# Two attention layers and two gated MLPs on one core: the kernel rebuilt around chunks of 512 tokens

## The chip, the cores and the metric

The kernel runs on one core of one Trainium2 chip. The core has a matrix engine (TensorE, PE in the profile; its weight loads are shown apart as PEld), a vector engine (VectorE, DVE), an engine for functions of one variable (ScalarE, ACT), a general engine (GpSimd, POOL) and an engine that mostly issues transfers (SyncE, SP). Matrix products land in PSUM, a small memory of eight banks per partition, a bank holding 512 fp32 numbers; everything else lives in SBUF, and the inputs lie in HBM. The metric is the device time of one execution in microseconds (us).

## The reference, cut to what matters

The input x has 2048 tokens of 1024 features in bf16. A linear attention layer (A) and a gated MLP (B) are applied in turn, twice, with the same weights, each on the layernorm of x and added to it.

```python
def _A_ref(x, wqkv, wo):                      # H = 32 heads of 32 features
    q, k, v = split(x @ wqkv)                 # 1024 -> 3 x 1024
    phi = lambda t: jnp.where(t > 0, t + 1, jnp.exp(t)) + 1e-6
    pq, pk = phi(q), phi(k)
    kv = jnp.einsum("bhsd,bhse->bhde", pk, v) # 32x32 per head, over all tokens
    z = jnp.einsum("bhsd->bhd", pk)
    num = jnp.einsum("bhqd,bhde->bhqe", pq, kv)
    den = jnp.einsum("bhqd,bhd->bhq", pq, z)[..., None] + 1e-6
    return (num / den) @ wo

def _B_ref(x, W_gate, W_up, W_down):          # F = 3584
    gate, up = x @ W_gate, x @ W_up
    gate = gate * (gate > 0)
    return (gate * up) @ W_down

x = x + _A_ref(_layernorm(x), A_wqkv, A_wo)
x = x + _B_ref(_layernorm(x), B_W_gate, B_W_up, B_W_down)
x = x + _A_ref(_layernorm(x), A_wqkv, A_wo)
x = x + _B_ref(_layernorm(x), B_W_gate, B_W_up, B_W_down)
```

## The kernel before

The tokens are cut into 16 tiles of 128. The residual x is held in SBUF in fp32 for the whole run (`x_sb`); it is read in bf16 and cast at the start, and cast back and written at the end.

`_layernorm_T` (lines 17 to 44) normalizes one tile: statistics on DVE (L25, L27), variance plus epsilon on DVE (L29), a square root on ACT (L30), a reciprocal on DVE (L31), the normalized tile in bf16 on DVE (L33), eight 128x128 transposes on PE (L39), and two copies out of PSUM, one on ACT (L42) and one on DVE (L44).

`_phi` (lines 47 to 53) makes max(t, 0) + exp(min(t, 0)) + 1e-6 out of a PSUM tile in four instructions, DVE, ACT, DVE, ACT.

`_layer_A` has two stages. In the first, for each tile, k and v are made from the transposed tile and a weight slab of 4 MB (L112, 32 matmuls of 128x512 per tile), k goes through `_phi`, and v is copied out with a column of ones behind each group of 128 features (L120). `kv_step` then makes, for eight groups of 128 features, pk times v together with pk's sums (L92), and adds them to an fp32 sum in SBUF on DVE (L97). At the stage's end the sum is masked to the 32x32 blocks of the heads (L128), and a matrix `zrep` is built that holds the sums in the same block form (L131). In the second stage, for each chunk of 512 tokens and each group of 128 features, q is made (L165), goes through `_phi`, and `nd_step` makes numerator and denominator by one matmul each per 256 tokens (L150, L152); ACT adds epsilon to the denominator (L155), DVE takes its reciprocal (L157) and multiplies (L158). Eight groups make a chunk, and the chunk is multiplied by wo and added to x (L179, L183). The weights of the second stage lie in another pool, which is loaded when the first stage's is given up.

`_layer_B` takes the tokens in two halves of 1024. For each half, gate and up are made for 28 blocks of 128 features (L227), the gate goes through a Relu on ACT (L231), and DVE multiplies (L232). Then W_down is applied in seven groups of four feature blocks; after each group the partial sums are added to x on DVE (L243, L247). Weights stream through pools with two buffers; the loads are issued on SP's queue and on ACT's. The first half's eight tiles are normalized before its matmuls, the second half's within the first half's down stage.

The order of the instructions on each engine is the scheduler's of the tile framework: the order of the program is a priority, and an instruction that is ready may be taken ahead of one that isn't. Buffers of a pool are given again when their last reader is done; a load or a write into one waits for that.

## Time and profile before

| | |
|---|---|
| time, median of 3 runs | 1966.81 us (1965.41 to 1966.97) |
| profiled execution, span from the first to the last instruction | 1957.3 us |
| what lies around the span (median less span) | 9.5 us |
| mean granted TensorE clock | 0.960 of full speed |
| PE, DVE, ACT busy | 1747.4, 1133.1, 502.6 us |
| HBM read, written | 109.05 MB, 4.19 MB |

The profile is one execution, with a record for each instruction; the page has no time of its own for that execution other than its span, so the time of the runs is set beside it. A row of a group gives line, engine, operation, output and inputs with their shapes, count, then busy us, mean ns of one, then the idle time of the engine just before and what ended it. A row of a window gives start and end, length, busy us and count for PE, PEld, DVE, ACT and POOL, the granted clock, the share of time that the 16 DMA engines were busy, and GB/s. Matmuls overlap in a pipeline, so the mean of one (379 ns for 128x512) is longer than their pace.

### The profile page before, as it was taken

Reading aid. Unit: us, or ns where it says so; the run is one execution under the profiler, and the core shown is the slowest. Engines: PE = TensorE matmul, PEld = TensorE weight load, DVE = VectorE, ACT = ScalarE, POOL = GpSimd, SP = SyncE. Lnnn points to the kernel's source line nnn. Section 1 sums busy time; section 2 is a strip of 40 time slices with the busy share of each in tenths; the row PEclk is TensorE's granted clock in tenths of the full one; section 3 lists DMA queues with packets and bytes.
Section 4 is the critical chain, followed back from the end, with each engine's and each line's share of the span. In section 5 each row is a group of like instructions: output and inputs, shape, how many; then the busy total and the mean of one; then the engine's idle time right before and its main releaser. Section 6 shows DMA issues by size and latency. Waiting matters only on the chain.

```text
span 1957.3 us, 21219 instructions
## 1 busy us (share of the span) xinstructions
PE 1747.4 (89%) x8282; PEld 809.6 (41%) x8448; DVE 1133.1 (58%) x1863; ACT 502.6 (26%) x853; POOL 21.2 (1%) x54
## 2 busy tenths in 40 slices
PE   6995777699999999999979957666999999999998
PEld 3452333244444444444434423333444444444443
DVE  7856999841117822117786679998322288212277
ACT  5852433321110011110067524333111100111100
POOL 1000000000000000000000000000000000000000
PEclk9998888899999999999999978998999999999999
DMA  4002000042222222211120020002332313232112
GB/s 172 1 1 86 0 1 1 2 135 80 76 75 67 84 71 80 76 54 52 57 86 2 1 86 1 1 1 62 90 86 66 87 65 114 81 85 66 44 65 87
DMA packets 142886, 114.64 MB, mean 59 GB/s; under 512 B 3520, under 2 KB 118208, under 8 KB 142784
## 3 DMA queue, kind: packets, MB, share of 16 engines
q1 hardware_dynamic: 72448, 58.73, 9.6%
q10 hardware_dynamic: 70336, 54.53, 9.1%
q8 instruction: 66, 1.08, 0.2%
q14 instruction: 36, 0.29, 0.0%
HBM read 109.05 MB, written 4.19 MB: 58 GB/s over the span
## 4 chain that ended last, share of the span: by engine, by line
PE 72%; DVE 16%; ACT 4%; issue 4%; DMA 3%; POOL 0%; SPq 0%; POOLq 0%; ACTq 0%; DVEq 0%
PE pu L227 19%; PE pg L227 19%; PE ps L243 19%; DVE rd L157 8%; PE ps L112 7%; PE ps L179 4%; DVE oT L158 2%; DVE m L51 1%; DVE m L49 1%; DMA xin<-in_A_x_dram 1%; DMA wq<-in_A_wqkv_dram 1%; PE ps L165 1%; ACT L50 1%; DVE xn L33 1%; DVE stats L25 1%
## 5 line engine op out<-in xcount | busy, mean ns | idle before, releaser
L232 DVE TENSOR_TENSOR hT<-pu,rg 128x512 bf16<-128x512 f32 x224 | 154.8, 691 | 598.4 <-PE pu L227 581.7
L227 PE MATMUL pg<-xnT_h,wg 128*128 128x512 bf16 x1758 | 421.5, 379 | 3.6 <-DVE xnT_h L44 1.9
L227 PE MATMUL pu<-xnT_h,wu 128*128 128x512 bf16 x1752 | 421.2, 379 | 2.2
L243 PE MATMUL ps<-wd,hT 128*128 128x512 bf16 x1754 | 387.4, 379 | 2.0
L247 DVE TENSOR_TENSOR x_sb<-x_sb,ps 128x512 f32<-128x512 f32 x448 | 305.8, 687 | 68.6 <-PE ps L243 66.7
L231 ACT ACTIVATE rg<-pg 128x512 f32<-128x512 f32 x224 | 133.7, 597 | 623.9 <-PE pg L227 597.8
L227 PEld LDWEIGHTS <-wg 128*128 128x128 bf16 x1792 | 174.9, 98 | 210.9 <-issue 2.5
L227 PEld LDWEIGHTS <-wu 128*128 128x128 bf16 x1792 | 175.1, 98 | 209.8
L243 PEld LDWEIGHTS <-hT 128*128 128x128 bf16 x1792 | 174.8, 98 | 208.6
L112 PE MATMUL ps<-wkv,xnT 128*128 128x512 bf16 x995 | 228.0, 381 | 8.5 <-ACT va L120 3.4
L157 DVE RECIPROCAL rd<-rd 128x256 f32<-128x256 f32 x128 | 220.4, 1736 | 5.9 <-ACT rd L155 5.6
L179 PE MATMUL ps<-wo,oT 128*128 128x512 bf16 x500 | 142.9, 431 | 73.2 <-DVE m L51 46.7
L165 PE MATMUL ps<-xnT,wq 128*128 128x512 bf16 x499 | 142.8, 426 | 62.1 <-DVE m L51 39.9
L112 PEld LDWEIGHTS <-xnT 128*128 128x128 bf16 x1024 | 99.8, 98 | 123.7 <-issue 11.9
L50 ACT ACTIVATE m<-m 128x512 f32<-128x512 f32 x128 | 79.1, 628 | 133.2 <-DVE m L49 130.5
L49 DVE TENSOR_SCALAR m<-ps 128x512 f32<-128x512 f32 x128 | 85.5, 670 | 47.2 <-PE ps L165 32.9
L165 PEld LDWEIGHTS <-wq 128*128 128x128 bf16 x512 | 52.7, 105 | 132.2 <-issue 77.9
L179 PEld LDWEIGHTS <-oT 128*128 128x128 bf16 x512 | 54.9, 109 | 126.2 <-issue 68.2
L51 DVE SCALAR_TENSOR_TENSOR m<-ps,m 128x512 f32<-128x512 f32 x128 | 84.3, 667 | 26.9 <-ACT m L50 26.6
L25 DVE BATCH_NORM_STATS2 stats<-x_sb 128x6 f32<-128x512 f32 x128 | 83.8, 672 | 0.6 <-POOL x_sb L297 0.5
L155 ACT ACTIVATE rd<-nd,eps 128x256 f32<-128x256 f32 x128 | 57.9, 468 | 97.5 <-DVE oT L158 54.1
L42 ACT ACTIVATE xnT_h<-tp 128x512 bf16<-128x512 bf16 x32 | 19.1, 597 | 216.6 <-PE tp L39 191.4
(43 smaller groups left out, 745.1 us busy)
## 6 DMA issues: line engine op xcount, KB each, us to landing
wg<-in_B_W_gate_dram SPq DMA_DIRECT2D x56, 512.0 KB, 3.8
wu<-in_B_W_up_dram ACTq DMA_DIRECT2D x56, 512.0 KB, 5.0
wd<-in_B_W_down_dram SPq DMA_DIRECT2D x16, 1024.0 KB, 5.3
wd<-in_B_W_down_dram ACTq DMA_DIRECT2D x12, 1024.0 KB, 5.4
wkv<-in_A_wqkv_dram ACTq DMA_DIRECT2D x8, 512.0 KB, 9.0
wkv<-in_A_wqkv_dram SPq DMA_DIRECT2D x8, 512.0 KB, 8.2
wo<-in_A_wo_dram ACTq DMA_DIRECT2D x16, 256.0 KB, 5.4
wq<-in_A_wqkv_dram SPq DMA_DIRECT2D x16, 256.0 KB, 5.4
```

What stands on the lines that cost most here:

```text
L25: nc.vector.bn_stats(out=stats[:, c, :], in_=xr[:, c, :])
L49: nc.vector.tensor_scalar(out=m, in0=ps, scalar1=0.0, scalar2=None, op0=ALU.min)
L51: nc.vector.scalar_tensor_tensor(out=m, in0=ps, scalar=0.0, in1=m, op0=ALU.max, op1=ALU.add)
L112: nc.tensor.matmul(ps, lhsT=xnT[:, kt, st * P:(st + 1) * P], rhs=wkv[:, kt, c * NW:(c + 1) * NW], start=(kt == 0), stop=(kt == KT - 1))
L157: nc.vector.reciprocal(out=rd, in_=rd)
L165: nc.tensor.matmul(ps, lhsT=wq[:, kt, g * P:(g + 1) * P], rhs=xnT[:, kt, sc * NW:(sc + 1) * NW], start=(kt == 0), stop=(kt == KT - 1))
L179: nc.tensor.matmul(ps, lhsT=oT[:, g, j * P:(j + 1) * P], rhs=wo[:, g, n2 * NW:(n2 + 1) * NW], start=(g == 0), stop=(g == G - 1))
L227: nc.tensor.matmul(p_, lhsT=w_[:, kt, fi * P:(fi + 1) * P], rhs=xnT[:, kt, sc * NW:(sc + 1) * NW], start=(kt == 0), stop=(kt == KT - 1))
L231: nc.scalar.activation(out=rg, in_=pg, func=ACT.Relu)
L232: nc.vector.tensor_tensor(out=hT[:, ft, sc * NW:(sc + 1) * NW], in0=pu, in1=rg, op=ALU.mult)
L243: nc.tensor.matmul(ps, lhsT=hT[:, fg * FG + k, j * P:(j + 1) * P], rhs=wd[:, k, n2 * NW:(n2 + 1) * NW], start=(k == 0), stop=(k == FG - 1))
L247: nc.vector.tensor_tensor(out=xs, in0=xs, in1=ps, op=ALU.add)
```

## The change

The program is written anew around chunks (`q`) of 512 tokens, four tiles each.

- **Weights** of all layers pass through one ring of seven buffers of 1 MB, in a fixed plan, all issued on SP's queue. x is read, and the result written, on ACT's queue. In the MLP each chunk of 512 tokens reads all three matrices.
- **Order by hand**: each block of about eight wide matmuls ends in a tick, and layernorms, transposes, kv sums and denominators are put behind a given number of ticks, so that they stand between blocks of matmuls on every engine. The layernorm of a chunk is put into the chunk before it, that of the next layer's first chunk into the layer before.
- **Layernorm**: 1/sqrt(v + eps) is made by ACT as exp(-0.5 ln(v + eps)); one copy of 1024 columns out of PSUM per tile, on DVE and ACT in turn.
- **phi**: exp on ACT straight from PSUM; then min(e, 1) + 1e-6 and max(t, 0) + e on DVE: three instructions.
- **kv sums** stay in three PSUM banks over all 16 tiles. The masked kv is transposed and multiplied into wo (`fold_wo`), so the output is one product of pq/den with the folded matrix; only the denominator is a matmul of its own, 512 columns wide, and its reciprocal is exp(-ln(den + eps)) on ACT, multiplied into pq on DVE in place.
- **Down sums** of the MLP stay in four PSUM banks over all 28 feature blocks and are added to x once; in the last layer the sum is written as bf16 and stored at once.

```diff
+    def load_to(self, n):
+        while self.loaded < min(n, len(self.plan)):
+            name, src = self.plan[self.loaded]
+            t = self.pool.tile([P, 8, NW], BF16, tag="w")
+            self.nc.sync.dma_start(out=t[:, 0:src.shape[1], :], in_=src)
+            self.tiles[name] = t
+            self.loaded += 1
...
+    def free_before(self, name):
+        i = next(k for k, e in enumerate(self.plan) if e[0] == name)
+        self.load_to(i + self.depth)
...
+    def at(self, delay, fn):
+        self.n += 1
+        self.tasks.append((self.now + delay, self.n, fn))
...
+        self.xnTp = pool("xnT", 4)
+        self.wring = pool("wring", 7)
+        self.slab = pool("slab", 8)
+        self.ep = pool("ep", 3)
+        self.xio = pool("xio", 3)
...
+        self.ps = pool("ps", 4, space=PSUM)
+        self.ps3 = pool("ps3", 3, space=PSUM)
+        self.pst = pool("pst", 1, space=PSUM)
...
+    def ln_norm(self, layer, t):
...
+        nc.scalar.activation(out=rstd, in_=mv[:, 1:2], func=ACT.Ln, bias=self.eps5[:, 0:1])
+        nc.scalar.activation(out=rstd, in_=rstd, func=ACT.Exp, scale=-0.5)
+        xn = self.xnp.tile([P, D], BF16, tag="xn")
+        nc.vector.tensor_scalar(out=xn, in0=src, scalar1=mv[:, 0:1], scalar2=rstd[:, 0:1],
+                                op0=ALU.subtract, op1=ALU.mult)
...
+    def ln_later(self, layer, q, first, step, lag):
+        for j in range(QT):
+            t = q * QT + j
+            def norm(t=t):
+                xn = self.ln_norm(layer, t)
+                self.later.at(lag, lambda: self.ln_turn(layer, t, xn))
+            self.later.at(first + j * step, norm)
...
+    def phi(self, ps, out):
+        e = self.ep.tile([P, NW], F32, tag="e")
+        nc.scalar.activation(out=e, in_=ps, func=ACT.Exp)
+        nc.vector.tensor_scalar(out=e, in0=e, scalar1=1.0, scalar2=1e-6, op0=ALU.min, op1=ALU.add)
+        nc.vector.scalar_tensor_tensor(out=out, in0=ps, scalar=0.0, in1=e,
+                                       op0=ALU.max, op1=ALU.add)
...
+        def kv_step(t):
+            for g in range(G):
+                b, i = divmod(g, 3)
+                nc.tensor.matmul(kv[b][:, i * (P + 1):(i + 1) * (P + 1)],
+                                 lhsT=pk[t][:, g * P:(g + 1) * P], rhs=va[t][:, g, :],
+                                 start=(t == 0 and i == 0), ...)
...
+            if l == 0 and q == 0:
+                for j in range(QT):
+                    self.ln_turn(l, j, self.ln_norm(l, j))
+            if q + 1 < self.NQ:
+                self.ln_later(l, q + 1, 2, 4, 2)
...
+        def den(sc, g):
+            p = pq[sc, g // 4][:, g % 4, :]
+            ps = self.ps3.tile([P, NW], F32, tag="b")
+            nc.tensor.matmul(ps, lhsT=zrep[:, g, :], rhs=p, start=True, stop=True)
+            r = self.ep.tile([P, NW], F32, tag="e")
+            nc.scalar.activation(out=r, in_=ps, func=ACT.Ln, bias=self.eps6[:, 0:1])
+            nc.scalar.activation(out=r, in_=r, func=ACT.Exp, scale=-1.0)
+            nc.vector.tensor_tensor(out=p, in0=p, in1=r, op=ALU.mult)
...
+        def fold_wo():
...
+                    nc.tensor.matmul(ps, lhsT=kvT[:, g, :], rhs=w[:, g, :], start=True, stop=True)
+                    dst = T[g // 2][:, g % 2, n2 * NW:(n2 + 1) * NW]
+                    if g % 2:
+                        nc.scalar.activation(out=dst, in_=ps, func=ACT.Copy)
+                    else:
+                        nc.vector.tensor_copy(out=dst, in_=ps)
...
+                self.phi(ps, pq[sc, g // 4][:, g % 4, :])
+                later.at(lag, lambda g=g: den(sc, g))
+                later.tick()
...
+        ring.free_before((l, "o0"))
+        later.at(3, finish_kv)
+        q_units(0, 4)
+        fold_wo()
+        ring.free_before((l, "q0"))
+        q_units(1, 2)
+        out_units(0)
+        self.ln_later(last_ln, 0, 2, 4, 3)
+        q_units(2, 2)
+        out_units(1)
+        q_units(3, 2)
+        ring.free_before((l, "o1"))
+        out_units(2)
+        out_units(3)
...
+            if q + 1 < self.NQ:
+                self.ln_later(l, q + 1, 8, 8, 4)
+            elif not final:
+                self.ln_later(l + 1, 0, 8, 8, 4)
...
+            for n2 in range(D // NW):
+                acc = [self.ps.tile([P, NW], F32, tag="a", name=f"acc{l}_{q}_{n2}_{j}")
+                       for j in range(QT)]
+                for dg in range(4):
+                    ring.free_before((l, q, "d", n2, dg))
+                    wd = ring.get((l, q, "d", n2, dg))
+                    for j in range(QT):
...
+                            nc.tensor.matmul(acc[j], lhsT=hT[ft // 4][:, ft % 4, j * P:(j + 1) * P],
+                                             rhs=wd[:, k, :], start=(ft == 0),
+                                             stop=(ft == self.FT - 1))
...
+        nc.scalar.preload_act_table_set("natural_log_exp_and_others")
+        for t in range(3):
+            self.load_x(t)
+        self.layer_A(0, 1)
+        self.layer_B(1, False)
+        self.layer_A(2, 3)
+        self.layer_B(3, True)
```

499 lines of the change are left out of this document (241 added, 258 removed).

## The prediction

> **What bounds the kernel now.** I read the totals and the strip of slices first, then the stages as a table of windows, then the groups of instructions and the waits of the slow stages, then the DMA rows.
>
> ```profile
> PE 1747.4 (89%) x8282; PEld 809.6 (41%) x8448; DVE 1133.1 (58%) x1863; ACT 502.6 (26%) x853; POOL 21.2 (1%) x54
> ...
> PE   6995777699999999999979957666999999999998
> ...
> DVE  7856999841117822117786679998322288212277
> ...
> PE 72%; DVE 16%; ACT 4%; issue 4%; DMA 3%; POOL 0%; SPq 0%; POOLq 0%; ACTq 0%; DVEq 0%
> ```
>
> PE's strip has two troughs, slices 4 to 8 and 23 to 28, and there DVE stands at 9. The chain of waits (last line) is 72% PE, and DVE's 16% is nearly all of the rest. The next table cuts the span where the PE's line of code changes (start:end and length in us, busy us of each engine with instruction counts, granted clock, DMA share, GB/s).
>
> ```profile
> 16.40:150.60 134.20, 128.28 (x746) 65.42 (x760) 101.77 (x217) 93.02 (x145) 9.07 (x20) 1.00 0.08 23
> 150.60:390.50 239.90, 164.05 (x636) 70.15 (x649) 206.39 (x297) 78.25 (x142) 0.00 (x0) 0.82 0.05 18
> 390.50:395.70 5.20, 2.76 (x32) 2.12 (x33) 4.64 (x12) 3.53 (x7) 0.00 (x0) 1.00 0.96 254
> 395.70:981.90 586.20, 582.29 (x2721) 267.72 (x2774) 247.98 (x392) 74.91 (x132) 0.00 (x0) 1.00 0.25 74
> 981.90:995.00 13.10, 3.94 (x24) 2.43 (x24) 13.01 (x36) 3.34 (x8) 0.20 (x3) 0.74 0.83 321
> 995.00:1122.00 127.00, 123.22 (x718) 62.89 (x733) 87.47 (x183) 90.27 (x138) 1.73 (x13) 1.00 0.00 1
> 1122.00:1360.50 238.50, 157.26 (x658) 68.58 (x668) 208.18 (x301) 78.93 (x144) 0.00 (x0) 0.87 0.05 18
> ...
> 1365.20:1952.00 586.80, 582.23 (x2720) 267.64 (x2774) 252.17 (x400) 74.78 (x132) 7.28 (x7) 1.00 0.26 80
> ```
>
> In order: the k and v stage of attention (134 and 127 us), the q and output stage (240 and 239 us), the layernorm before an MLP (5 us, the second one alike), the MLP (586 us, twice), and the layernorm before the second attention layer (13 us). PE is busy for 99% of the MLP and for 66 to 68% of the q stages. So the MLP is at the pace of the matmuls, and what can be won lies in the q stages, at the joints between layers and at the two ends of the span. The pace comes from a window inside the MLP that holds nothing but 128x512 matmuls, and from two short bursts of narrow ones (start, length, count):
>
> ```profile
> 450.00:500.00 50.00, 49.79 (x229) 22.69 (x232) 10.38 (x15) 8.36 (x14) 0.00 (x0) 1.00 0.29 85
> ```
>
> ```profile
> 998.97 0.61 PE L39 MATMUL tp<-ident,xn 128*128 128x128 bf16 x8
> ...
> 1121.84 0.64 PE L92 MATMUL kp<-va,pk 128*128 128x129 bf16 x8
> ```
>
> There are 232 weight loads in 50 us (some matmul records are missing, so I count loads), so a 128x512 matmul costs **0.2155 us**. One narrow matmul by itself lasts about 0.22 us, so eight in 0.61 or 0.64 us come at a pace of (0.61-0.22)/7 = 0.055 and 0.060 us.
>
> **The matmuls that stay, by stage.** The MLP keeps 2688 wide ones a layer: 896 each for gate, up and down. With 128 layernorm transposes this is 2688 x 0.2155 + 128 x 0.055 = 586.3 us, and 584.6 in the last layer, which prepares no successor (96 transposes): nothing is won against 586, as the row says it can't be. The k and v stage keeps 512 wide, 128 of 129 columns and now 96 transposes (one block of four tiles is prepared earlier): 110.3 + 7.7 + 5.3 = 123.3 us. The q stage changes: 256 wide for q and 256 for the output stay, 128 matmuls of 256 columns for numerator and denominator (64 wide ones' worth) become 32 wide for the denominator alone, the numerator moves into 16 wide ones that multiply the masked kv into wo, and 40 transposes are added: 560 x 0.2155 + 40 x 0.055 = 122.9 us. The PE's floor is 2 x (123.3 + 122.9) + 586.3 + 584.6 = **1663.3 us**. That the MLP's partial sums stay in PSUM takes away 320 of its 448 adds on DVE, at 0.69 us; they lay beside matmuls and are costed at nothing, because DVE is idle for more than half of that stage.
>
> **What the other engines ask of the q stage.** These are groups with count, busy us and mean ns of one:
>
> ```profile
> L157 DVE RECIPROCAL rd<-rd 128x256 f32<-128x256 f32 x128 | 220.4, 1736 | 5.9 <-ACT rd L155 5.6
> ...
> L49 DVE TENSOR_SCALAR m<-ps 128x512 f32<-128x512 f32 x128 | 85.5, 670 | 47.2 <-PE ps L165 32.9 <-PE ps L112 12.6 <-ACT pq L53 0.9
> L51 DVE SCALAR_TENSOR_TENSOR m<-ps,m 128x512 f32<-128x512 f32 x128 | 84.3, 667 | 26.9 <-ACT m L50 26.6
> L25 DVE BATCH_NORM_STATS2 stats<-x_sb 128x6 f32<-128x512 f32 x128 | 83.8, 672 | 0.6 <-POOL x_sb L297 0.5
> L50 ACT ACTIVATE m<-m 128x512 f32<-128x512 f32 x128 | 79.1, 628 | 133.2 <-DVE m L49 130.5 <-DVE rstd L29 1.7
> ...
> L33 DVE TENSOR_SCALAR xn<-x_sb,mv,rstd 128x1024 bf16<-128x1024 f32 x64 | 51.3, 803 | 0.0
> ...
> L53 ACT ACTIVATE pq<-m,eps 128x512 bf16<-128x512 f32 x64 | 45.5, 719 | 62.1 <-DVE m L51 62.1
> ...
> L30 ACT ACT_TABLE_LOAD x27 | 34.6, 1283 | 7.0 <-DMA xin<-in_A_x_dram 5.4 <-DVE rstd L29 1.2
> L50 ACT ACT_TABLE_LOAD x26 | 33.4, 1283 | 14.2 <-DVE rstd L31 6.2 <-DVE m L49 4.8 <-POOL x_sb L297 1.9
> ...
> L44 DVE COPY xnT<-tp 128x512 bf16<-128x512 bf16 x32 | 13.3, 416 | 0.2
> ...
> L306 DVE CAST xo<-x_sb 128x1024 bf16<-128x1024 f32 x8 | 5.5, 694 | 0.3
> ```
>
> The reciprocal is 220 us of DVE, all of it in the two troughs of 478 us, where DVE is busy 414. It goes. In its place a unit of q (one group of 128 features, 512 tokens) costs PE 9 x 0.2155 = **1.94 us**. On ACT it costs an Exp and a second Exp at about 628 ns (L50) and one Ln with a bias operand, nearest L53, 719: 1.98 us, less what back-to-back instructions overlap. On DVE it costs the minimum-and-add, now from SBUF and not from PSUM, bounded by 416 (L44, half the length of L306's 694 or less) and 670 (L49); I take 450, nearest L306. Then the maximum-and-add, 667, and the product of pq and the reciprocal, bounded by L51's 667 and the MLP's product of 691: 1.81 us in all, 2.03 at the dear end. So all three engines need nearly the same 1.8 to 2.0 us. The Trainium skill (VectorE: DVE Perf Modes, "The perf-mode tier table") has an fp32 tensor_scalar run at twice the rate from SBUF and not from PSUM; L306 against L49 agrees.
>
> A wait is added: the denominator matmul of unit g stands on PE right behind the matmuls of unit g+1 (a lag of two ticks), and needs unit g's phi: Exp, minimum, maximum, 0.63 + 0.45 + 0.67 = 1.75 us and about 0.3 us of handing on, against 1.72 us of the eight matmuls in front. It comes a few tenths late; behind it stand the matmuls of unit g+2, so the delay is PE's. I take 0.1 us for each of 24 such units (2.4), 2.5 for the fold (16 matmuls take 3.4 us, but their copies, eight on ACT at 0.6 and eight on DVE at 0.67, take 5.4), and 3 for the four layernorm tiles put into this stage (each 2 x 0.67 + 0.2 + 0.80 of DVE). **That is 8 us a layer**, bounds 2 (the scheduler moves matmuls forward, as it already does here) and 25 (2.5 us a unit, 18 in all, and 7 for the rest).
>
> **Joints and ends.** The 5 us before the MLP and the 13 us before the second attention go, since a block's tiles are normalized while the block before it is multiplied. Such a layernorm lands in the k and v stage, too: DVE has 16 units of 1.72 us a block, and is asked for 8 x 1.12 + 4 x 2.4 + about 2 = 20.6 of 27.6 us. I allow 3 us a stage (0 to 10), the second stage before being 2 over its matmuls, and 1 us per MLP (0 to 4). At the start four tiles are normalized in a row before their matmuls stand in the order: the first one lands at 5 us (row below), four times 2.9 us of DVE with its waits for ACT, and 1.9 for the last transposes and copies make 18.5 us (12 if matmuls move forward, 24 if x lags as the second piece did), with 2 us for cold matmuls (1 to 3). At the end 0.69 us for the last add and 3 us for a smaller store, in all 4.5 (3.5 to 6).
>
> ```profile
> 0.74 4.25 DMA xin<-in_A_x_dram
> 5.74 6.53 DMA xin<-in_A_x_dram
> ```
>
> **The transfers.** Weights of the MLP are now read for each 512 tokens, not for each 1024: 4 x 22.0 = 88 MB a layer over 586 us, 150 GB/s, on SP's queue alone, in pieces of 1 MB with 1 KB rows. One piece serves 6.7 us of matmuls and five pieces are ahead.
>
> ```profile
> 4.00:8.00 4.00, 0.00 (x0) 0.00 (x0) 2.34 (x5) 1.49 (x2) 0.20 (x1) 1.00 1.01 404
> ...
> 390.00:396.00 6.00, 3.01 (x34) 2.24 (x35) 5.44 (x13) 4.31 (x7) 0.00 (x0) 1.00 0.89 235
> ...
> wd<-in_B_W_down_dram SPq DMA_DIRECT2D x16, 1024.0 KB, 5.3
> ...
> wkv<-in_A_wqkv_dram SPq DMA_DIRECT2D x8, 512.0 KB, 8.2
> ```
>
> The DMA engines moved 404 GB/s of 4 KB rows and, 0.89 busy, 235 GB/s of 512 B rows (264 if full). 150 GB/s of 1 KB rows is between 0.37 and 0.57 of what they can do; I cost it at nothing.
>
> **Sum.** 1663.3 + 18.5 + 2 + 2 x 3 + 2 x 8 + 2 x 1 + 4.5 = 1712.3 us of span. The profiled execution's span is 1957.3, the median of the runs 1966.8, so 9.5 us lie around a span; the profile gives no other time of its own. **1722 us.** With all low ends 1693, with all high ends 1784.
>
> **Rivals.**
> (a) *The tables swap.* Exp and Ln alternate in the q units. Before, Sqrt and Exp swapped 53 times at 1283 ns. Should each Ln and each Exp behind it load a table, a unit costs ACT 1.98 + 2 x 1.28 = 4.5 us, and 64 units add 64 x (4.5 - 1.94) = 164: 1886. Against it: one set that is loaded by name at the start and never left. The Trainium skill (ScalarE: Activation LUTs, "Table sets: the hidden batching unit") puts exp and ln into that one set; no run here shows it yet.
> (b) *The chain isn't covered.* If PE waits for a whole unit (phi 1.75, denominator 0.4, Ln, Exp and product 2.0, less 1.94 of its own), 64 x 2.2 = 141: 1863. For it: DVE's 16% of the chain, which lie in that stage. Against it: four PSUM banks instead of three.
> (c) *The clock stays low.* The q stages' row shows 0.82 and 0.87 granted where PE idles, 1.00 elsewhere. At 0.82 the 122.9 us become 150: 54 for both, 1776. Against it: PE would idle a few tenths of a us at a time, as in the k and v stage with its clock of 1.00. The Trainium skill (TensorE: Matmul & The Clock Gate, "A second HAM failure mode: psum-queue depth-cycling") warns that short idles from cycling through PSUM banks drop the clock; the k and v stage, which cycles through three, disagrees.
> (d) *SP's one queue paces the MLP: slower than before.* If pieces go one after the other and each takes as long as L83's half-megabyte piece, 8.2 us, the 176 pieces take 176 x 8.2 = 1443 us in place of 1172: 1993. It decides from 8.05 us a piece, where 176 x (8.05 - 6.66) eats the gain of 245. For it: that row; against it: 5.3 us for a whole megabyte, and that the 8.2 was taken behind seven other pieces and x.
>
> **How the numbers follow.** Forecast 80%, with (c) inside its range at 5%; (a) 6%, (b) 5%, (d) 4%. The range is 1692 to 1785, which leaves out (a), (b), (d) and a little of the forecast. A measurement of this kernel can tell about 0.2% from no change; all but (d) lie further below that, so faster 0.95, the same 0.01, slower 0.04.
>
> **What would show it.** Right: PE busy 95% or more outside the first 20 us; q stages of 125 to 140 us at a clock near 1.00; MLPs of 586 to 590 us with the DMA share at about 0.5; one or two table loads; no layernorm gap at the joints. Wrong: a row of PE waiting for a weight piece in the MLP (d), many table loads (a), q units at 4 us (b), a q stage with its clock below 0.9 (c), or a start of over 25 us.

## The result and the profile after

The changed kernel takes **1696.41 us** (median of 4 runs, 1696.14 to 1698.89) against 1966.11 us for the kernel before in the same comparison: ratio 0.8632, 95% interval 0.8617 to 0.8646. It is 270 us faster. The forecast was 1722.

The totals, two rows of the strip of slices and the first line of the chain of waits of the changed kernel:

```profile
PE 1675.2 (99%) x8304; PEld 778.6 (46%) x8304; DVE 595.0 (35%) x1002; ACT 392.5 (23%) x723; POOL 21.2 (1%) x54
...
PE   6999999999999999999999999999999999999999
...
PEclk9999999999999999999999999999999999999999
...
PE 95%; DVE 3%; ACT 1%; DMA 1%; issue 0%; DVEq 0%; ACTq 0%
```

The two troughs of PE are gone; only the first slice is not full. The chain of waits puts 3% on DVE, where it was 16%. (The clock column reads 1.00 in the first slice too, where the first six matmuls of 512 columns take 2.74 us, and six of them 1.46 us a little later; the last section comes back to this.)

The same kernel, cut where PE's line of code changes (start:end and length in us, busy us of PE, weight loads, DVE, ACT and GpSimd with counts, granted clock, DMA share, GB/s):

```profile
0.00:14.19 14.19, 1.82 (x17) 1.76 (x18) 7.42 (x21) 2.78 (x7) 4.12 (x17) 1.00 0.93 303
14.19:141.41 127.22, 125.28 (x747) 63.72 (x745) 62.99 (x123) 49.97 (x98) 14.77 (x21) 1.00 0.26 83
141.41:268.46 127.05, 126.09 (x612) 56.08 (x610) 109.52 (x190) 69.14 (x128) 0.00 (x0) 1.00 0.13 42
268.46:855.76 587.30, 587.30 (x2817) 270.17 (x2816) 140.53 (x216) 80.42 (x152) 0.93 (x7) 1.00 0.46 149
855.76:978.70 122.94, 122.94 (x729) 62.54 (x728) 50.17 (x91) 46.10 (x82) 1.42 (x9) 1.00 0.11 35
978.70:1105.75 127.05, 126.08 (x611) 56.08 (x609) 109.53 (x190) 69.14 (x128) 0.00 (x0) 1.00 0.13 42
1105.75:1691.20 585.45, 585.45 (x2785) 268.27 (x2783) 114.11 (x170) 74.98 (x130) 0.00 (x0) 1.00 0.45 145
1691.20:1694.70 3.50, 0.24 (x2) 0.00 (x0) 0.69 (x1) 0.00 (x0) 0.00 (x0) 1.00 0.22 75
```

In order: the start, k and v, q and output, MLP, k and v, q and output, MLP, tail. The q stages went from 239.9 and 238.5 us to 127.05 each; that alone is 224 of the 270 us. The joints of 5 and 13 us have no row any more. The MLPs stayed where they were, though they now read their weights twice as often (149 GB/s where it was 74).

What a unit of q costs on ACT and DVE, from the groups of instructions of the changed kernel (count, busy us, mean ns of one, idle before), with the only table load:

```profile
L174 ACT ACTIVATE e<-ps 128x512 f32<-128x512 f32 x128 | 76.2, 595 | 137.1 <-PE ps L229 116.4 <-PE ps L298 16.3 <-DVE xn L137 2.2
L175 DVE TENSOR_SCALAR e<-e 128x512 f32<-128x512 f32 x128 | 54.9, 429 | 57.3 <-ACT e L174 56.3
L176 DVE SCALAR_TENSOR_TENSOR pq<-ps,e 128x512 bf16<-128x512 f32 x64 | 44.2, 690 | 2.1
L273 DVE TENSOR_TENSOR pq<-pq,r 128x512 bf16<-128x512 bf16 x64 | 43.8, 689 | 6.1 <-ACT r L272 3.7
L271 ACT ACTIVATE r<-ps,eps 128x512 f32<-128x512 f32 x64 | 43.4, 686 | 3.3 <-PE ps L269 2.4
L272 ACT ACTIVATE r<-r 128x512 f32<-128x512 f32 x64 | 40.0, 633 | 1.7
...
L399 ACT ACT_TABLE_LOAD x1 | 1.3, 1283 | 0.7 <-PEq L437 0.7
```

ACT: 595 + 686 + 633 = 1.91 us a unit. DVE: 429 + 690 + 689 = 1.81 us. PE's nine matmuls: 1.94 us.

### The profile page after: what moved, and what is told of

It is laid out like the page before. It is cut to its first block, busy times and chain, and to the rows that moved or that the text cites. A ratio compares the mean times of both kernels' runs of the same rounds, so it can differ in the third digit from the quotient of the medians.

```text
span 1694.7 us, 19592 instructions
## 1 busy us (share of the span) xinstructions
PE 1675.2 (99%) x8304; PEld 778.6 (46%) x8304; DVE 595.0 (35%) x1002; ACT 392.5 (23%) x723; POOL 21.2 (1%) x54
## 3 DMA queue, kind: packets, MB, share of 16 engines
q8 instruction: 65, 1.06, 0.3%
## 4 chain that ended last, share of the span: by engine, by line
PE 95%; DVE 3%; ACT 1%; DMA 1%; issue 0%; DVEq 0%; ACTq 0%
PE acc L380 23%; PE pg L363 23%; PE pu L363 23%; PE ps L229 13%; PE ps L298 5%; PE ps L311 5%; PE tp L153 2%; PE kv L204 1%; PE ps L269 1%; DMA xin<-in_A_x_dram 1%; DVE stats L130 1%; DVE x L315 0%; DVE xn L137 0%; DVE pq L273 0%; ACT r L271 0%
## 5 line engine op out<-in xcount | busy, mean ns | idle before, releaser
L363 PEld LDWEIGHTS <-t 128*128 128x128 bf16 x3584 | 349.5, 98 | 416.3
L363 PE MATMUL pg<-xnT,t 128*128 128x512 bf16 x1792 | 423.3, 379 | 0.0
L363 PE MATMUL pu<-xnT,t 128*128 128x512 bf16 x1792 | 423.3, 379 | 0.0
L380 PE MATMUL acc<-t,hT 128*128 128x512 bf16 x1792 | 388.1, 379 | 0.0
L229 PE MATMUL ps<-t,xnT 128*128 128x512 bf16 x1024 | 230.4, 380 | 0.0
L298 PE MATMUL ps<-xnT,t 128*128 128x512 bf16 x512 | 121.6, 379 | 0.2
L311 PE MATMUL ps<-T,pq 128*128 128x512 bf16 x512 | 113.4, 379 | 0.0
L174 ACT ACTIVATE e<-ps 128x512 f32<-128x512 f32 x128 | 76.2, 595 | 137.1 <-PE ps L229 116.4
L298 PEld LDWEIGHTS <-t 128*128 128x128 bf16 x512 | 49.7, 98 | 56.1 <-issue 1.7
L175 DVE TENSOR_SCALAR e<-e 128x512 f32<-128x512 f32 x128 | 54.9, 429 | 57.3 <-ACT e L174 56.3
L130 DVE BATCH_NORM_STATS2 stats<-x 128x6 f32<-128x512 f32 x96 | 65.4, 691 | 2.4
```

The costliest lines, as they stand in the source:

```text
L130: nc.vector.bn_stats(out=stats[:, c, :], in_=src[:, c * fmax:(c + 1) * fmax])
L174: nc.scalar.activation(out=e, in_=ps, func=ACT.Exp)
L175: nc.vector.tensor_scalar(out=e, in0=e, scalar1=1.0, scalar2=1e-6, op0=ALU.min, op1=ALU.add)
L229: nc.tensor.matmul(ps, lhsT=self.xnT[l, q][:, kt, j * P:(j + 1) * P], rhs=w[:, kt, :], start=(kt == 0), stop=(kt == KT - 1))
L298: nc.tensor.matmul(ps, lhsT=w[:, kt, (g % 4) * P:(g % 4 + 1) * P], rhs=self.xnT[l, sc][:, kt, :], start=(kt == 0), stop=(kt == KT - 1))
L311: nc.tensor.matmul(ps, lhsT=pq[sc, g // 4][:, g % 4, j * P:(j + 1) * P], rhs=T[g // 2][:, g % 2, n2 * NW:(n2 + 1) * NW], start=(g == 0), s ...
```

## The experiments

Each kernel below is the changed kernel with one edit, unless it is said to start from another. Times are medians; the comparisons ran on different chips, where the kernel before took 1961 to 1976 us, so both the time and the ratio to the kernel before are given.

**1. The denominator's reciprocal back on DVE.**

```diff
-            nc.scalar.activation(out=r, in_=ps, func=ACT.Ln, bias=self.eps6[:, 0:1])
-            nc.scalar.activation(out=r, in_=r, func=ACT.Exp, scale=-1.0)
+            nc.scalar.activation(out=r, in_=ps, func=ACT.Identity, bias=self.eps6[:, 0:1])
+            nc.vector.reciprocal(out=r, in_=r)
```

> The changed kernel with one part undone: the reciprocal of the denominator is again ACT's Identity with epsilon and DVE's reciprocal, everything else as changed. Theory (the reciprocal on DVE was what held the q stages): a unit of q costs DVE 0.43 + 0.69 + 2 x 1.74 + 0.69 = 5.3 us against 1.94 of PE; if the output blocks shelter part of it the q stages grow by some 80 us each, if not by 107: 1858 to 1910 us, DVE busy 90% or more in both q stages. Rival (the order by hand and the folded wo carry the gain, and the reciprocal hides beneath the matmuls): under 1760.

Measured: 1847.10 us, ratio 0.9365 (0.9338 to 0.9392), 151 us more. The first line of its chain of waits, and the window of its first q lines:

```profile
PE 81%; DVE 16%; issue 2%; DMA 1%; ACT 0%; ACTq 0%
```

```profile
141.40:322.90 181.50, 122.38 (x514) 49.88 (x522) 176.81 (x182) 50.22 (x86) 0.00 (x0) 0.86 0.09 29
```

DVE is busy 177 of 181.5 us: it is the bound again, and its 16% of the chain is back, with the clock at 0.86. From the first q matmul to the end of the MLP it is 789.1 us (141.40 to 930.46) against 714.35 in the changed kernel: 75 us a layer. That is under the theory's low end, 81 a layer, so the time lies 11 us below its range. The scheduler puts a part of the output blocks into the MLP (between 322.88 and 345 us the two kinds of matmul alternate on PE); that they cost less there is the likely reason and not shown by itself.

**2. The line that loads the table set by name, taken out.**

```diff
-        nc.scalar.preload_act_table_set("natural_log_exp_and_others")
```

> The changed kernel without the one line that loads the table set of exp and ln by name at the start. The program then has a table load before nearly every Ln and every Exp behind it, 244 in all. Theory: this is rival (a) of the prediction come true; a unit of q costs ACT 0.69 + 0.63 + 0.60 + 2 x 1.28 = 4.5 us against 1.94 of PE. With 1.72 us of shelter per output unit the q stages grow by some 35 us each, without any by 82: 1766 to 1860 us, ACT the busiest engine there. Rival (the loads run while ACT would wait anyway): within 15 us of 1696.

Measured: 1862.36 us, ratio 0.9442 (0.9415 to 0.9470), 166 us more. The table loads of the q units among its groups, and its first q stage:

```profile
L271 ACT ACT_TABLE_LOAD x60 | 77.0, 1283 | 1.1
L272 ACT ACT_TABLE_LOAD x60 | 77.0, 1283 | 1.1
```

```profile
155.50:357.70 202.20, 146.05 (x601) 59.91 (x611) 107.97 (x190) 172.68 (x208) 0.00 (x0) 0.86 0.09 26
```

Nearly every Ln and every Exp behind it loads a table, in the q units (L271, L272) and likewise in the layernorm, 244 loads in all. ACT is busy 173 us of the q stage where it was 69. Of the 166 us, 152 lie in the two q stages (202.2 and 203.8 us against 127.05 each) and 14 in the time before the first q matmul, where the loads of the layernorm fall into the first k and v stage; the MLPs and the second k and v stage stand as they were. The time is 2 us above the range that was expected. The rival (a) of the prediction was real; one line keeps it out.

**3. The kernel before with both reciprocals as exp(-ln).** Nothing else of the change: no new chunks, ring, fold or schedule.

```diff
-    nc.vector.tensor_scalar(out=rstd, in0=mv[:, 1:2], scalar1=1e-5, scalar2=None, op0=ALU.add)
-    nc.scalar.activation(out=rstd, in_=rstd, func=ACT.Sqrt)
-    nc.vector.reciprocal(out=rstd, in_=rstd)
+    nc.scalar.activation(out=rstd, in_=mv[:, 1:2], func=ACT.Ln, bias=eps5[:, 0:1])
+    nc.scalar.activation(out=rstd, in_=rstd, func=ACT.Exp, scale=-0.5)
...
-                        nc.scalar.activation(out=rd, in_=nd[:, 1, :], func=ACT.Identity,
-                                             bias=eps[:, 0:1])
-                        nc.vector.reciprocal(out=rd, in_=rd)
+                        nc.scalar.activation(out=rd, in_=nd[:, 1, :], func=ACT.Ln,
+                                             bias=eps[:, 0:1])
+                        nc.scalar.activation(out=rd, in_=rd, func=ACT.Exp, scale=-1.0)
...
+    nc.scalar.preload_act_table_set("natural_log_exp_and_others")
```

> The kernel before with one part of the change alone: both reciprocals as exp(-ln) on ACT (layernorm and denominator), with the table set loaded by name, 1 table load instead of 53. Theory (reciprocal and table swaps hold the q stages): DVE falls to 0.67 + 0.67 + 2 x 0.40 = 2.1 us a unit, but ACT rises to 0.63 + 0.72 + 2 x (0.47 + 0.42) = 3.1 us against 2.16 of PE, so the q stages go from 240 to some 165 us each, 10 of it the wait for wq: about 1815 us (1790 to 1850), more than half of the whole gain of 270. Rival (the gain comes of the rebuilt order, PSUM use and folding): above 1870.

Measured: 1783.61 us, ratio 0.9043 (0.9017 to 0.9069). So (1 - 0.9043) / (1 - 0.8632) = **70% of the gain is reached by this part alone**. That is 6 us better than the range that was expected. The window of its first q stage, with the wait for wq before it and the joint behind it, and what its q matmuls waited for (us in total, times, longest):

```profile
147.90:321.50 173.60, 151.49 (x748) 71.70 (x764) 122.47 (x251) 93.49 (x232) 0.00 (x0) 0.95 0.15 49
```

```profile
PE ps L164 <- DMA wq<-in_A_wqkv_dram: 21.9, 9, 10.1
```

DVE has 122 of 174 us to do and no longer sets the pace. The edit also takes the table loads from 53 to 1. Of the 176 us by which the profiled span is shorter than that of the kernel before (1781.3 against 1957.3), 169 lie in the two q stages (148.8 and 149.6 us, from the first q matmul to the first of the MLP, against 235.2 and 232.6), which held only 7 of the 53 loads each, 9 us of ACT; so the reciprocal is the likely main part; no run separates the two. What is left over the changed kernel, 87 us (86.6 of span), stands by its matmuls in these places (first matmul of a stage to first matmul of the next): 29 us in the start and the two k and v stages with the wait for wq at their end, 44 in the two q stages (against 127.05 each), 13 in the MLPs with their joints.

**4. The layernorm of a layer's first block back at the layer's start.** Three joints get it back.

```diff
-            if l == 0 and q == 0:
+            if q == 0:
                 for j in range(QT):
                     self.ln_turn(l, j, self.ln_norm(l, j))
...
-        self.ln_later(last_ln, 0, 2, 4, 3)
...
+            if q == 0:
+                for j in range(QT):
+                    self.ln_turn(l, j, self.ln_norm(l, j))
             if q + 1 < self.NQ:
                 self.ln_later(l, q + 1, 8, 8, 4)
-            elif not final:
-                self.ln_later(l + 1, 0, 8, 8, 4)
```

> The changed kernel with the layernorm of a layer's first 512 tokens back at the layer's own start in the program (three joints), not in the layer before. Theory (the joints' gaps of 13 and 5 us were the price of that place): 4 tiles x 2.9 + 1.9 = 13.5 us of DVE chain per joint, partly drawn forward by the scheduler: 5 to 13 us each, 1711 to 1736 us, with a PE gap at each joint. Rival (x is final long before, so that the scheduler draws these layernorms forward by itself and the order by hand brings nothing): 1696 to 1702.

Measured: 1713.28 us, ratio 0.8687 (0.8661 to 0.8712): 16.9 us more. PE's timeline at the first joint (start, length, idle before and its releaser) and the granted clock behind it:

```profile
267.28 0.61 PE L153 MATMUL tp<-ident,xn 128*128 128x128 bf16 x8
268.82 0.61 PE L153 MATMUL tp<-ident,xn 128*128 128x128 bf16 x8 [0.93 <-DVE xnT L157]
270.54 0.61 PE L153 MATMUL tp<-ident,xn 128*128 128x128 bf16 x8 [1.11 <-DVE mv L132]
272.36 1.01 PE L153 MATMUL tp<-ident,xn 128*128 128x128 bf16 x8 [1.22 <-DVE xnT L157]
274.49 3.57 PE L363 MATMUL pg<-xnT,t 128*128 128x512 bf16 x8 [1.11 <-ACT xnT L159]
```

```profile
274.49:278.00 3.51, 3.51 (x9) 1.27 (x9) 2.97 (x6) 0.99 (x4) 0.00 (x0) 0.50 0.00 0
```

This joint costs its gaps (4.4 us) and then a second time: the first eight matmuls of the MLP take 3.57 us at a clock of 0.50, where the changed kernel needs 1.89. By stages, the q stage is 5.3 us longer and the MLP behind it 2.0, and the third joint, before the second MLP, costs the same. The second joint, before the second attention layer, costs only about 1.2: there the scheduler puts k matmuls between the transposes of the tiles, PE has a single gap of 0.93 us, and the clock doesn't fall. (The rest, 0.7 us, lies in the start.)

**5. The denominator three units behind, not two.** Chunks 1 to 3; chunk 0 has four already.

```diff
-        q_units(1, 2)
+        q_units(1, 3)
```

and so for chunks 2 and 3.

> The changed kernel with the denominators of the second to fourth chunk put three ticks behind their q unit, not two. Theory (the added wait of the prediction: the denominator matmul stands on PE a few tenths before phi is done): in the changed kernel's trace the steps from a q unit or an output unit to a denominator matmul are 0.08 to 0.38 us too long, 1.8 us in each q stage; with one more unit in between they vanish: 3 to 4 us less, 1692 to 1693. Rival (the pace there is set by ACT and DVE, which are asked for the same 1.8 to 2.0 us a unit, and the wait only moves to a buffer): 1695.5 to 1697.

Measured: 1692.73 us (1692.49 to 1693.40), ratio 0.8603 (0.8570 to 0.8637), 3.7 us less. The first q stage:

```profile
142.22:267.31 125.09, 123.90 (x599) 57.37 (x609) 108.86 (x190) 69.54 (x128) 0.00 (x0) 1.00 0.14 43
```

125.09 against 127.05: 1.96 us a layer, 0.08 for each of 24 units. In its chain of waits DVE has 0% where the changed kernel has 3%.

**6. The numerator not folded.** Each unit multiplies by the masked kv behind its denominator, and the output matmuls read wo as loaded.

```diff
+            num = self.ps3.tile([P, NW], F32, tag="b")
+            nc.tensor.matmul(num, lhsT=kvm[:, g, :], rhs=p, start=True, stop=True)
...
-            nc.vector.tensor_tensor(out=p, in0=p, in1=r, op=ALU.mult)
+            nc.vector.tensor_tensor(out=p, in0=num, in1=r, op=ALU.mult)
...
-        fold_wo()
...
-                                         rhs=T[g // 2][:, g % 2, n2 * NW:(n2 + 1) * NW],
+                                         rhs=ring.get((l, f"o{n2}"))[:, g, :],
```

> The numerator is no longer folded into the output weights: each unit of q multiplies its pq with the masked kv (a 128x512 matmul behind the denominator's), DVE multiplies that sum from PSUM with the reciprocal, and the output matmuls read the output weights as loaded. All else stays. Theory (the fold saves only PE time): 32 wide matmuls a layer instead of 16 for the fold and 8 transposes of the masked kv: 16 x 0.2155 - 8 x 0.055 = +3.0 us, less the 1.3 us for which the fold's copies held up PE in the profile of the changed kernel: +1.7 us a layer, about 1700 us (1697 to 1704). Rival (the fold also keeps PSUM free: two sums a unit from three buffers, one of which is held through Ln, Exp and product, 2.3 us, against 2.15 us of PE a unit): PE waits 0.5 us or more a unit, 64 units, 1730 us or more, and the clock in the q stages falls below 1.00.

Measured: 1698.37 us (1697.94 to 1700.31), ratio 0.8630 (0.8609 to 0.8651).

```profile
143.66:271.46 127.80, 127.36 (x620) 58.63 (x618) 106.03 (x182) 64.88 (x119) 0.00 (x0) 1.00 0.09 26
```

The q stage is 0.75 us longer with 3.0 us more matmuls in it, so 2.25 us of something else went with the fold. That PE had waited for the fold's copies is the likely reading and not shown by itself: PE's idle time in the stage falls by only 0.5 us (0.96 to 0.44). The fold brings 1.5 us over both layers together; the clock stays at 1.00 and PSUM isn't short without it. (This profile's first q stage begins at 143.66 and not at 141.41, because of a longer start, on which the last section has more.)

**7. The MLP's down sums closed for each weight piece and added in SBUF.** 256 adds on DVE in place of 64.

```diff
-                acc = [self.ps.tile([P, NW], F32, tag="a", name=f"acc{l}_{q}_{n2}_{j}")
-                       for j in range(QT)]
...
+                        acc = {j: self.ps.tile([P, NW], F32, tag="a", name=f"acc{l}_{q}_{n2}_{dg}_{j}")}
...
-                                             rhs=wd[:, k, :], start=(ft == 0),
-                                             stop=(ft == self.FT - 1))
+                                             rhs=wd[:, k, :], start=(k == 0),
+                                             stop=(k == 6))
...
-                        if dg < 3:
-                            continue
-                        if not final:
+                        if not final or dg < 3:
```

> The changed kernel with one part undone: the MLP's down sums are closed after each piece of seven feature blocks and added to x in SBUF, 256 adds in the two layers in place of 64. Theory (this part was costed at nothing, because the adds lie beside matmuls): 192 more adds of 0.69 us, one per 1.5 us of PE, and no change: 1695 to 1698. Rival (closing the sums makes PE wait for free PSUM banks, so that the PSUM sums do carry some of the gain): over 1702.

Measured: 1696.42 us (1696.37 to 1698.76), ratio 0.8625 (0.8597 to 0.8654). The adds in its groups:

```profile
L385 DVE TENSOR_TENSOR x<-x,acc 128x512 f32<-128x512 f32 x224 | 154.0, 687 | 170.4 <-PE acc L379 168.0 <-remote 0.8
```

DVE works 132 us more (192 adds of 0.687) and the time doesn't move: half of the adds that this part of the change saved (448 before, 64 after) come back at no cost, so it is worth nothing here.

**8. A shorter ring in the MLP, first try.** Four buffers of the ring were to be held through each MLP by tiles that are written at its start and read at its end.

```diff
+        held = []
+        for i in range(4):
+            h = self.wring.tile([P, 8, NW], BF16, tag="w", name=f"held{l}_{i}")
+            nc.gpsimd.memset(h[:, 0, 0:8], 0.0)
+            held.append(h)
...
+        for h in held:
+            g = self.small.tile([P, 8], BF16, tag="held_out")
+            nc.gpsimd.tensor_copy(out=g, in_=h[:, 0, 0:8])
```

> The changed kernel with four of the ring's seven buffers held back while each MLP runs, so that three are left. Theory (a piece lands 5.4 us after its issue and the ring's depth alone hides it): the next up piece can only be issued when the last gate piece is done, 1.7 us before the block's end, and is needed 1.7 us after it: 5.4 - 3.4 = 2.0 us late for each of 56 blocks, 112 us more; the down pieces stay hidden with 12 us ahead: about 1810 us (1770 to 1870). Rival (a piece alone in the queue lands sooner, in 3.4 us or less, and the depth is more than is needed): under 1720.

Measured: 1697.72 us (1696.56 and 1698.89), ratio 0.8629 (0.8585 to 0.8673). The edit didn't do what it says. GpSimd's timeline:

```profile
240.56 0.10 POOL L350 MEMSET held<- 128x8 bf16 x1 [157.22 <-remote]
240.72 0.48 POOL L400 COPY g<-held 128x8 bf16<-128x8 bf16 x1
```

The copies that should have kept the buffers until the MLP's end depend on nothing but the writes, and ran with them before the MLP had begun. This run says nothing about the ring.

**9. A shorter ring, second try.** The ring is split: four buffers for attention, three for the MLP.

```diff
-        self.wring = pool("wring", 7)
+        self.wring = pool("wring", 4)
+        self.wring_b = pool("wring_b", 3)
```

with each piece taken from the ring of its stage and loaded when that ring has room.

> The ring of seven weight buffers is split: four for attention's pieces, three for the MLP's. Theory (the transfers cost nothing because five pieces are ahead, not because they are short): in the changed kernel a 1 MB piece takes 5.2 to 5.8 us from issue to landing. With three buffers the next block's up piece is issued only when the gate piece of this block is read for the last time, 1.72 us before the block's end, and is wanted 1.72 us after the next block's start: 5.4 - 1.72 - 1.72 = 2.0 us late, 56 times, so the MLP stages together are 112 us longer and the time is about 1808 us (1780 to 1830), with PE waiting for a transfer 56 times. Rival (a piece alone on the queue lands in 3.4 us or less, the 5.4 us being time in line behind other pieces): below 1720 us, and three buffers would have been enough. The attention stages hardly move in either case (4 pieces are all that they hold at a time).

Measured: 1728.36 us (1727.38 to 1729.20), ratio 0.8780 (0.8760 to 0.8801), 32 us more: between the two. SP's issue of an up piece, and PE's matmuls around its use (the timeline joins matmuls of one kind that follow each other):

```profile
280.69 0.37 SPq L34 DMA_DIRECT2D t<-in_B_W_up_dram  x1
```

```profile
282.23 3.40 PE L374 MATMUL pg<-xnT,t 128*128 128x512 bf16 x15
286.19 1.90 PE L374 MATMUL pu<-xnT,t 128*128 128x512 bf16 x8 [0.56 <-DMA t<-in_B_W_up_dram]
```

The transfer is as the theory had it: issued at 280.69 and in use at 286.19, 5.5 us with nothing ahead of it. What the theory missed stands in front of the wait: 15 gate matmuls and not 8, and so in front of each of the 48 waits. The scheduler moved 7 matmuls of the next gate group forward, which cover 7 x 0.2155 = 1.5 of the 2.0 us; by the times 32 / 48 = 0.67 us is left in each of the 48 blocks where PE waits. The first block of each of the 8 chunks has no such wait. The seven buffers are worth 32 us, less than a third of what the theory gave them.

**10. An earlier start, on top of lag 3.** The identity is cast on GpSimd, four tiles of x are prefetched and not three, two of them on SP's queue.

```diff
-        nc.vector.tensor_copy(out=self.ident, in_=ident_f)
+        nc.gpsimd.tensor_copy(out=self.ident, in_=ident_f)
...
-        self.xio = pool("xio", 3)
+        self.xio = pool("xio", 4)
...
-        self.nc.scalar.dma_start(out=xin, in_=self.x_v[:, t, :])
+        (self.nc.sync if t < 4 and t % 2 == 0 else self.nc.scalar).dma_start(out=xin, in_=self.x_v[:, t, :])
```

> The changed kernel with lag 3 and a quicker start: the identity matrix is cast on GpSimd instead of DVE (in the trace the first transposes wait 1.4 us for it), and four tiles of x instead of three are fetched ahead, every second one on SP's queue ahead of the weights. Theory (the start is 14.2 us and 5.7 us of holes behind it, because the second and third tile land at 7.7 us among 4 MB of weights and the fourth at 16.5): 3 to 6 us less from the start and 3 to 4 from the lag: 1687 to 1691. Rival (the chain of four layernorms on DVE sets the start, whenever x lands): the lag's part alone, 1692 to 1694.

Measured: **1691.75 us** (1691.72 to 1691.77), ratio 0.8599 (0.8571 to 0.8627): the fastest version of the study, but only 1.0 us under lag 3, just outside both the theory's range and the rival's. PE's first instructions, and DVE's at the same time:

```profile
7.28 1.04 PE L153 MATMUL tp<-ident,xn 128*128 128x128 bf16 x8 [7.28 <-DVE xn L137]
12.38 1.01 PE L153 MATMUL tp<-ident,xn 128*128 128x128 bf16 x8 [4.06 <-DVE xnT L157]
13.19 2.34 PE L229 MATMUL ps<-t,xnT 128*128 128x512 bf16 x5
```

```profile
8.66 1.88 DVE L130 BATCH_NORM_STATS2 stats<-xin 128x6 f32<-128x512 bf16 x3 [1.44 <-DMA xin<-in_A_x_dram]
...
11.69 0.64 DVE L157 COPY xnT<-tp 128x1024 bf16<-128x1024 bf16 x1
```

The first transposes come 4.3 us earlier than in the changed kernel (11.58), the first matmul of k only 1.0 us (14.19). The transposed tile was ready for its copy at 8.3, but in DVE's order the statistics of tile 2 stand ahead, and DVE waited for that tile until 8.66.

**11. The first tiles' copies on ScalarE, and each tile transposed right before its own matmuls.** On top of the version above.

```diff
-        if self.n_evac % 2:
+        if self.n_evac % 2 and (layer or q):
...
+                    if c == 0 and first:
+                        self.ln_turn(l, j, xn.pop(j))
+                        if j + 2 < QT:
+                            xn[j + 2] = self.ln_norm(l, j + 2)
```

> The kernel with the denominator three units behind and the earlier start (the last look gave 1691.75 us), and now each of the first four tiles is transposed right before its own matmuls, not all four ahead of the first matmul, and ScalarE, which is idle there, takes the first tiles out of PSUM in place of DVE. Theory (the start waits for DVE's order: the copy of the first transposed tile stood behind the statistics of tiles 2 and 3): the first k matmul comes at about 9.2 us instead of 13.19, tiles follow every 2.5 us, and the time is 1688 to 1690 us. Rival (the statistics of four tiles, in a row on DVE, set the end of the start in any order): the first matmul is earlier but the matmuls behind it wait, and the time stays within 1 us of 1691.75.

Measured: 1699.58 us (1699.43 to 1701.04), ratio 0.8636 (0.8615 to 0.8656): 7.8 us slower than the version above, against theory and rival. PE's first matmuls of k, and ACT's copy of the first tile:

```profile
13.30 3.60 PE L233 MATMUL ps<-t,xnT 128*128 128x512 bf16 x8 [4.81 <-ACT xnT L159]
```

```profile
12.22 1.02 ACT L159 ACTIVATE xnT<-tp 128x1024 bf16<-128x1024 bf16 x1 [0.93 <-DVE mv L132]
```

The same wait on another engine: ACT's order has the Ln of a later tile, and the issue of a transfer of x, ahead of the copy, and that Ln waits 3.2 us for DVE's statistics, which wait for a tile that hasn't landed. The copy of a tile transposed by 8.5 us starts at 12.22. The second group of k matmuls comes at 20.65, for the same reason. With matmuls between the tiles, each such wait is now PE's, and the matmuls stay at half their pace for longer: the first three groups of eight take 3.60, 3.59 and 3.40 us, the last one from 26.21, and only the fourth, at 31.22, takes 1.90. In the changed kernel the pace is full from 16.75 on. An idle engine's order can be as full of waits as a busy one's.

## Why the prediction was right, and where it was off

Forecast and measurement by the terms of the sum, in us:

| term | forecast | measured | difference |
|---|---|---|---|
| start, cold matmuls, first k and v stage (18.5 + 2 + 3 + 123.3) | 146.8 | 141.41 | -5.4 |
| second k and v stage (123.3 + 3) | 126.3 | 122.94 | -3.4 |
| two q stages (122.9 + 8 each) | 261.8 | 254.1 | -7.7 |
| two MLPs (586.3 + 584.6 + 2) | 1172.9 | 1172.75 | -0.2 |
| tail | 4.5 | 3.5 | -1.0 |
| around the span | 9.5 | 1.9 | -7.6 |
| sum | 1721.8 | 1696.6 | -25.2 |

**The floor of 1663.3 us** was right: the MLPs run 1.0 and 0.9 us above it and the second k and v stage 0.4 below, with PE busy for the whole of their rows. The method, counting matmuls and taking their pace from a window that holds nothing else, carried 98% of the time.

The differences of the rows all point the same way: no row was forecast too cheap, so none hides another's error.

**"9.5 us lie around a span"** was, with the two q stages, the largest error, and it was wrong in kind. The run behind the profile of the changed kernel took 1696.57 us with a span of 1694.7; of the kernel before, one took 1962.56 with 1960.8 and another 1971.66 with 1969.9. In every run that has both numbers it is 1.7 to 2.0 us. By that, the 1957.3 of the profile before belongs to an execution of about 1959 us, whose own time is not on record, and most of the 9.5 was the spread between executions of that kernel (its runs here go from 1961 to 1976), not something that lies around each.

**The q stage's 8 us** were 4.1. The denominator's wait was sized well: 0.1 us for each of 24 units, measured 0.08 on average by lag 3. The other two terms were too dear: 2.5 for the fold and 3 for the four layernorm tiles are 2.2 together (125.09 with lag 3, less 122.9). The price of a unit was right on every engine: ACT 1.91 where 1.98 was forecast, DVE 1.81 where 1.81 was, with the minimum-and-add at 429 ns for 450. Three engines at 1.8 to 1.9 us a unit do run side by side.

**"I allow 3 us a stage"** for layernorm in the k and v stage: nothing was needed, and the 1 us per MLP was about what it took. The bound of zero would have been the reading of DVE's load, 20.6 of 27.6 us a block, that stood beside it. **The start** of 18.5 and 2 us was close in sum, but partly by luck: 141.41 less 123.3 is 18.1, cold matmuls included, so it was 2.4 too dear. The first k matmul came at 14.19, 4.3 earlier than forecast, since the scheduler did not keep the four tiles in a row but moved matmuls in behind the second one; behind it the stage took 3.9 us over its matmuls, with a hole of 1.9 us before the fourth tile, where 2 were forecast for cold matmuls. The two errors offset each other. It is still the one place where PE is idle for long, and experiments 10 and 11 show what holds it: the order of the engines' work against the order in which x lands.

**Two readings were wrong** and bore on nothing in the sum. DVE's 16% of the chain was 16 of the 28 that PE leaves, not nearly all of it (ACT and issue have 4 each, DMA 3). And the PSUM sums take away 384 of 448 adds, not 320: the changed kernel has 32 in each MLP.

**The transfers at nothing** were right, by the seven buffers (experiment 9). The issue rows of the changed kernel (KB each, us to landing):

```profile
t<-in_B_W_gate_dram SPq DMA_DIRECT2D x56, 1024.0 KB, 5.4
...
t<-in_B_W_down_dram SPq DMA_DIRECT2D x64, 896.0 KB, 5.8
```

Rival (d) needed 8.05 us a piece, one after the other; the pieces of the MLP take 5.2 to 5.8 (medians) with the DMA share at 0.46, and they overlap: 76 of the 192 weight pieces have the next one issued before they land. **Adds at nothing** were right, by experiment 7.

**The rivals.** (a) is what happens without one line. Its price was 164, all of it in the q units; experiment 2 has 152 there and 14 before them, so the price of a unit was nearly right, and that the whole comes to 166 is luck. The Trainium skill (ScalarE: Activation LUTs, "Table sets: the hidden batching unit") counts one load for an ln followed by an exp, since one set holds both; the trace agrees for the kernel that loads this set by name, and disagrees for the one that doesn't, which made 244 loads. (b), the uncovered chain, did not come: lag 2 covers all but 0.08 us a unit. (c) did not either: the clock reads 1.00 in both q stages. It did fall to 0.86 in experiments 1 and 2, where PE waits in each unit, so in these runs (c) goes with waits like those of (a) and (b) and isn't a case of its own.

**Where the gain is from.** The reciprocals leaving DVE, with the table loads that go with them, bring 189 us or 70% when they come first (experiment 3, on its chip). Taken back out of the changed kernel last, the denominator's reciprocal loses 151 us, or 56%; the rest of the change without it is worth 125 us (experiment 1 against the kernel before on its chip, with the layernorm's reciprocal still on ACT). The two parts overlap, so the share depends on the order, but it is more than half in both. The joints give about 16 us (experiment 4). The fold gives 1.5 and the PSUM sums of the MLP nothing. What remains, some 70 us, lies in the k and v and q stages of experiment 3's kernel: the late wq (22 us of PE's waiting), and q stages of 149 us with a clock of 0.97. Which of chunks, units of 512 tokens and lags brings how much of the latter wasn't taken apart.

## What to carry to other kernels

Price a stage by what each engine needs for one unit of it; where the slowest is DVE with a reciprocal (1.74 us for 256 columns, twice a unit), two steps on a less busy engine (here Ln and Exp on ACT, 0.69 and 0.63 us for 512) can be worth more than the reordering, provided that both functions come from one table set which is loaded by name. Place a dependent matmul so many units late that its producers' whole chain fits in between (here the matmuls of two units, 1.72 us each, for a chain of 1.7 us and its handing on; one unit fell 0.08 us short on average), and prepare the next stage's input while the last one multiplies, since a row of gaps can be paid again in a low clock. And take the time around a span from runs that give both numbers of the same execution, not from a profile and a median.

## What was not expected of the hardware

**A start with two lengths.** The changed kernel takes either about 1696.3 or about 1698.9 us, and so do variants of it. The profile of experiment 7 caught the longer one (span 1697.0), with its k and v stage ending at 143.68 and not at 141.41. A window of it, and the nearest one of the changed kernel:

```profile
22.14:26.20 4.06, 3.93 (x15) 1.67 (x15) 2.82 (x7) 1.80 (x4) 0.00 (x0) 0.71 1.08 354
```

```profile
21.04:25.30 4.26, 4.26 (x23) 1.95 (x21) 3.54 (x9) 2.71 (x7) 0.00 (x0) 1.00 1.09 353
```

15 matmuls in 4 us at a clock of 0.71 against 23 at 1.00 (a few transposes among both): after the short waits of the start the clock is low again in some executions and not in others. The low clock costs half of the difference; the other half is lost before 22 us, where the transposes of the third and fourth tile take 1.06 and 1.01 us and not 0.62 and 0.61, and the hole between them is 0.4 us longer. Experiment 6's profile, which also caught the longer start, reads 0.50 from 21.00 to 24.40 us, experiment 7's from 21.11 to 24.51, and 1.00 on both sides. Before its first full-speed stretch the column reads 1.00 as well, though the matmuls run at half pace there (in experiment 11, eight in 3.60 us from 13.30 to 16.90): in the first microseconds go by the matmuls' pace and not by the column. The Trainium skill (TensorE: Matmul & The Clock Gate, "Part 1: The HAM clock gate") says that the number of cold matmuls differs from run to run because the window in which activity is counted runs freely; the two lengths agree with that, and no run here shows the window itself.

**The kernel before can be the unsteady one.** In two comparisons its executions spread over 0.6 and 0.7% (9 from 1961 to 1974 us, 7 from 1962 to 1976, with mean clocks of 0.950 to 0.961), while each version of the changed kernel beside it stayed within 0.15% at 0.998 to 1.000. In the other two it spread over no more than 0.1% (4 and 3 runs), less than the four runs of the changed kernel with their 0.16%. That a PE which waits in every unit has its clock less in hand would fit, but isn't shown: experiments 1 and 2 wait in every unit, and their two runs each lie within 0.02%.
